# Decode attention: K of every query split by 32 dims x 4 key groups between VectorE and TensorE, V summed piece by piece

## The chip, the cores and the metric

The kernel runs on one core of a Trainium2 chip. The metric is the device time of one execution in microseconds (us), the median over several runs. The engines named below are TensorE (PE in the profile, PEld for its weight loads), VectorE (DVE), ScalarE (ACT), GpSimd (POOL) and SyncE (SP), whose queue issues all the large loads.

## The reference

One decode step for B = 2 sequences: layer norm, attention of one new token with 16 heads of 256 dims over a cache of 8192 keys, an output projection, and a bilinear feed-forward block. All is float32. The part that matters here:

```python
q = (layernorm(x) @ wq).reshape(B, 1, 16, 256).transpose(0, 2, 1, 3)
scores = jnp.einsum("bhqd,bhkd->bhqk", q, k_cache) * (256 ** -0.5)
p = softmax(scores, axis=-1)
o = jnp.einsum("bhqk,bhkd->bhqd", p, v_cache)
h = x + o.transpose(0, 2, 1, 3).reshape(B, 1, 4096) @ wo
h2 = h + ((layernorm(h) @ w_gate) * (layernorm(h) @ w_up)) @ w_down
```

k_cache and v_cache have the shape (2, 16, 8192, 256), so each of the 32 pairs of head and sequence (a "query", numbered i = 0 to 31 in the order of the loop) has 8 MB of K and 8 MB of V, and each of them is used for one vector only.

## The kernel before, in words

The host lays K, V and the weights out so that each load is one DMA of whole rows. For each query the program loads K into a tile of 128 partitions x 16384 values (64 KB a partition, line 98) and V into one of the same size (line 103). K has one buffer (`kbuf`, line 87), V has two (`vbuf`, line 88); the three fill most of the core's memory. Both loads are issued from SP's queue in the order K, V, K, V; a K load waits there until the readers of the K before it are done, and the V load behind it waits with it. The program order is as written (line 94), and each engine takes its own instructions in that order.

**V and the scores' layout.** The 8192 keys are cut into 4 groups of 2048 (`GK`), and the 256 dims into 8 pieces of 32 (`NO`, `R`). The scores of a query stand in PSUM as `s`, 128 x 2048: partition 32 g + r holds the scores of key group g, alike for all 32 values of r. There is one buffer of `s`. V's tile holds on partition 32 g + r, for each piece o, dim 32 o + r of the keys of group g, so that V times the probabilities `p` and a sum along the row gives the output, up to a sum over the four groups.

**K.** K's lower 128 dims lie one to a partition, with all 8192 keys in the row. TensorE multiplies them by the query as 32 equal columns, for each key group into its own 32 partitions of `s` (lines 266 to 272). For the upper 128 dims there are two ways. Where `by_vector(i)` holds (i a multiple of 3, and the last three; 13 of 32), they lie as V does, four pieces of 32 dims x 4 key groups; VectorE multiplies the first by the query's values (a scalar for each partition, from `qd`, line 256) and adds the other three to it with multiply-adds (line 261), the last in two halves, and TensorE then adds the 32 partitions of each group with a matmul by a block matrix of ones (line 275). The other 19 queries have the upper dims laid out as the lower and do them on TensorE, with c = 1 in line 267.

**The row of one query.** After the scores VectorE takes the maximum over `s` (line 322), ScalarE the exponential into `p` with its sum (line 324), and VectorE multiplies V by p and sums. Of three queries in turn, two do it with one multiply over all of V and one reduction (lines 346 and 347), the third with eight multiply-adds that sum as they go (line 350); `WIDE` says which, and from query 28 on all are of the second kind. ScalarE writes the query's columns for TensorE once a head (line 245).

**Around it.** Before the loop the first layer norm and the query projection run on wq, which is loaded ahead of the first K. In query 29, and again in query 31, `weights` (line 280) makes the factors that join the four groups' softmax sums, between the maximum and V. After the last V, the output projection and the feed-forward block run on weights that are loaded into the buffers of K and V as these come free (lines 359 and 366).

## Time and profile before

| | |
|---|---|
| median of 3 runs | 1303.92 us (1303.78 to 1304.15) |
| span of the profiled execution | 1302.1 us, from its first to its last instruction |
| what lies around the span, against the median | 1.8 us |
| mean granted TensorE clock | 0.647 of full speed |
| read from memory | 561.19 MB, 431 GB/s over the span |

The profiled execution has no time of its own beside the span; the 1.8 us are the difference between the median of the runs and that span. How to read the rows that the prediction shows: a group of the page gives line, engine, operation, what it writes and reads, the count, then busy time and mean duration in ns, then how long the engine stood idle just before and what ended that. A row of the timeline gives start, busy time, engine, line, operation and in brackets the idle time before it with its releaser; consecutive instructions of one kind are one row, and its time is then the sum. A row of the chain gives start, duration and the work. PEld rows are the weight loads, one ahead of each matmul, so that the distance from one to the next shows TensorE's pace. A float32 matmul shows as two instructions.

### The profile page before, as it was taken

Reading aid. Unit: us, or ns where it says so; the run is one execution under the profiler, and the core shown is the slowest. Engines: PE = TensorE matmul, PEld = TensorE weight load, DVE = VectorE, ACT = ScalarE, POOL = GpSimd, SP = SyncE. Lnnn points to the kernel's source line nnn. Section 1 sums busy time; section 2 is a strip of 40 time slices with the busy share of each in tenths; the row PEclk is TensorE's granted clock in tenths of the full one; section 3 lists DMA queues with packets and bytes.
Section 4 is the critical chain, followed back from the end, with each engine's and each line's share of the span. In section 5 each row is a group of like instructions: output and inputs, shape, how many; then the busy total and the mean of one; then the engine's idle time right before and its main releaser. Section 6 shows DMA issues by size and latency. Waiting matters only on the chain.

```text
span 1302.1 us, 5034 instructions
## 1 busy us (share of the span) xinstructions
PE 340.6 (26%) x2114; PEld 103.4 (8%) x2114; DVE 1075.6 (83%) x381; ACT 80.4 (6%) x111; POOL 2.2 (0%) x15
## 2 busy tenths in 40 slices
PE   2422112232202223211322311322311232221247
PEld 0100000000000000000000000000000000000013
DVE  0499879969987998899799879979987996987773
ACT  1100000000000000000000000000000000000000
POOL 0000000000000000000000000000000000000000
PEclk9866566666556666556666556666656666656668
DMA  9999999999999999999999999999999999999998
GB/s 419 419 449 421 447 423 445 425 443 427 439 429 441 425 441 427 437 428 437 433 435 433 434 435 435 435 433 437 431 439 431 437 429 435 433 433 433 433 425 358
DMA packets 11401, 561.50 MB, mean 431 GB/s; under 512 B 1266, under 2 KB 1652, under 8 KB 2292
## 3 DMA queue, kind: packets, MB, share of 16 engines
q1 hardware_dynamic: 11380, 561.20, 99.6%
q8 instruction: 16, 0.26, 0.1%
q14 instruction: 5, 0.04, 0.0%
HBM read 561.19 MB, written 0.00 MB: 431 GB/s over the span
## 4 chain that ended last, share of the span: by engine, by line
DMA 73%; PE 17%; DVE 10%; issue 1%; SPq 0%; DVEq 0%; ACT 0%; ACTq 0%
DMA k<-in_kc_dram 67%; PE s L269 13%; DVE k L261 6%; DMA v<-in_vc_dram 4%; PE s L275 3%; DVE v L350 3%; DMA wd_t<-in_wd_dram 2%; DVE k L256 1%; PE acc_ps L462 0%; SPq L366 0%; SPq L107 0%; PE u_ps L462 0%; SPq L98 0%; DVEq L256 0%; ACT tail L184 0%
## 5 line engine op out<-in xcount | busy, mean ns | idle before, releaser
L269 PE MATMUL s<-k,q 128*32 128x512 f32 x1632 | 248.3, 773 | 892.5 <-DMA k<-in_kc_dram 892.5
L346 DVE TENSOR_TENSOR v<-v,p 128x16384 f32<-128x16384 f32 x19 | 327.3, 17226 | 81.2 <-DMA v<-in_vc_dram 61.2
L347 DVE TENSOR_REDUCE oacc<-v 128x8 f32<-128x16384 f32 x19 | 327.2, 17220 | 0.7
L350 DVE SCALAR_TENSOR_TENSOR v<-v,p 128x2048 f32<-128x2048 f32 x104 | 231.1, 2288 | 31.8 <-ACT p L324 21.9
L269 PEld LDWEIGHTS s<-k,q 128*32 128x32 f32 x1632 | 66.7, 138 | 1070.9 <-issue 1069.2
L324 ACT ACTIVATE p<-s,nm 128x2048 f32<-128x2048 f32 x32 | 63.0, 1967 | 1131.7 <-DVE nm L322 1131.7
L322 DVE TENSOR_REDUCE nm<-s 128x1 f32<-128x2048 f32 x32 | 73.1, 2285 | 33.8 <-PE s L275 33.8
L261 DVE SCALAR_TENSOR_TENSOR k<-k,qd 128x2048 f32<-128x2048 f32 (+1 forms) x52 | 93.4, 1817 | 1.4
L275 PE MATMUL s<-k,block 128*128 128x512 f32 x104 | 48.1, 605 | 18.1 <-DVE k L261 18.1
L256 DVE TENSOR_SCALAR k<-k,qd 128x2048 f32<-128x2048 f32 x13 | 16.7, 1286 | 29.2 <-DMA k<-in_kc_dram 27.0
L275 PEld LDWEIGHTS s<-k,block 128*128 128x128 f32 x104 | 18.7, 189 | 49.0 <-DVE k L261 33.5
L138 DVE TENSOR_REDUCE sum_h_x<-xT 128x2 f32<-128x6 f32 x1 | 0.2, 159 | 20.6 <-ACT xT L165 20.6
L395 PE MATMUL acc_ps<-wo_t,oT 128*2 128x448 f32 x64 | 8.8, 646 | 11.4 <-DMA wo_t<-in_wo_dram 11.2
L201 PE MATMUL q_ps<-wq_t,xr 128*32 128x512 f32 x64 | 9.6, 753 | 1.4 <-ACT xr L184 1.1
L350 DVE DVE_READ_ACCUMULATOR v<-v,p 128x1 f32 x104 | 8.6, 83 | 0.0
L201 PE MATMUL ff_ps<-gu_t,xr 128*32 128x512 f32 (+1 forms) x32 | 6.4, 913 | 0.6 <-ACT xr L184 0.6
L324 ACT ACTIVATION_READ_ACCUMULATOR p<-s,nm 128x1 f32 x32 | 6.2, 193 | 0.0
L148 PE MATMUL total_x<-sum_h_x,ones 128*128 128x2 f32 x2 | 0.6, 348 | 21.1 <-DVE sum_h_x L141 21.1
L442 DVE TENSOR_SCALAR ve<-var_h 128x1 f32<-128x1 f32 x1 | 0.2, 158 | 6.4 <-PE var_h L440 6.4
L476 DVE COPY tail<-acc_ps 2x112 f32<-2x112 f32 x1 | 0.3, 261 | 5.5 <-PE acc_ps L462 5.5
L245 ACT ACTIVATE q<-qT 128x128 f32<-128x128 f32 x16 | 4.8, 298 | 0.0
L201 PE MATMUL u_ps<-gu_t,xr 128*32 128x512 f32 (+1 forms) x32 | 3.6, 544 | 0.0
(103 smaller groups left out, 66.0 us busy)
## 6 DMA issues: line engine op xcount, KB each, us to landing
wq_t<-in_wq_dram SPq DMA_DIRECT2D x1, 7172.0 KB, 19.6
wo_t<-in_wo_dram SPq DMA_DIRECT2D x1, 3584.0 KB, 16.5
wo_t<-in_wo_dram SPq DMA_DIRECT2D x1, 2688.0 KB, 22.5
gu_t<-in_B_w_gate_dram SPq DMA_DIRECT2D x1, 1792.0 KB, 28.0
gu_t<-in_B_w_up_dram SPq DMA_DIRECT2D x1, 1792.0 KB, 34.5
gu_t<-in_B_w_gate_dram SPq DMA_DIRECT2D x1, 1344.0 KB, 30.7
wd_t<-in_wd_dram SPq DMA_DIRECT2D x1, 1120.0 KB, 16.8
wo_t<-in_wo_dram SPq DMA_DIRECT2D x1, 896.0 KB, 24.2
```

The costliest lines, as they stand in the source:

```text
L201: nc.tensor.matmul(ps[32 * g : 32 * g + 32, : wide[g]], xs.rearrange("p b r -> p (b r)"), w[:, at : at + wide[g]], start=(c == 0), stop=(c ...
L245: nc.scalar.activation(q.rearrange("p c b r -> p (c b) r"), qT.rearrange("p k g j c b -> p (k g j) (c b)")[:, h, :, None] .to_broadcast([P ...
L256: nc.vector.tensor_scalar(upper[:, 0], upper[:, 0], qd[:, 0, i : i + 1], None, op0=ALU.mult)
L261: nc.vector.scalar_tensor_tensor(upper[:, 0, at], upper[:, o, at], qd[:, o, i : i + 1], upper[:, 0, at], op0=ALU.mult, op1=ALU.add,)
L269: nc.tensor.matmul(s[g * R : (g + 1) * R, at], q[:, c, i % B, :], kt[:, c, g, at], start=(c == 0), stop=(c == 1), skip_group_check=True,)
L275: nc.tensor.matmul(s[:, at], block, upper[:, 0, at], start=False, stop=True, skip_group_check=True,)
L322: nc.vector.tensor_reduce(nm[:, i : i + 1], s, axis=AX.X, op=ALU.max, negate=True)
L324: nc.scalar.activation(p, s, AF.Exp, bias=nm[:, i : i + 1], scale=1.0, accum_out=ls[:, i : i + 1])
L346: nc.vector.tensor_mul(v, v, p[:, None, :].to_broadcast([P, n, GK]))
L347: nc.vector.tensor_reduce(oacc[:, i, :n], v, axis=AX.X, op=ALU.add)
L350: nc.vector.scalar_tensor_tensor(v, v, 1.0, p, op0=ALU.mult, op1=ALU.mult, accum_out=oacc[:, i, o : o + 1])
L395: nc.tensor.matmul(acc_ps[32 * j : 32 * j + B, :], oT[:, h, c, :], wo_t[:, k * D : (k + 1) * D], start=(h < 2 and j > 0), stop=(h >= H - 2 ...
```

## The change

All of K now lies as V does: eight pieces of 32 dims x 4 key groups, for every query. Of the eight, the first `direct(i)` go to TensorE: two for most queries, one where i % 3 is 2 (queries 2, 5, ... 29). VectorE multiplies piece number `direct(i)` by the query's values and adds the remaining five or six to it, the last in two halves. TensorE multiplies its own pieces by a 128 x 128 matrix that holds the query's values in the blocks (`stationary`, built by ScalarE from `block`, one for each piece, ahead of each query), and closes with the matmul by ones on VectorE's sum. V is always done with eight multiply-adds, and `WIDE` is gone. `qd` now holds all eight pieces of each query, with eight small matmuls ahead of it instead of four. The sizes of the loads and their order are as before.

```diff
-WIDE = (8, 8, 0)
-def by_vector(i):
-    return i % 3 == 0 or i >= NQ - 3
+DIRECT = 2
+def direct(i):
+    return DIRECT - 1 if i % 3 == 2 else DIRECT
...
-        t = kbuf.tile([P, 2, G, GK], F32, tag="k", align_bytes=512, name=f"k_{h}_{b}")
+        t = kbuf.tile([P, NO, GK], F32, tag="k", align_bytes=512, name=f"k_{h}_{b}")
...
+    for c in range(2):
+        for o in range(G):
+            nc.tensor.matmul(
+                qd_ps[:, c * G + o, :].rearrange("p (n b) -> p n b", b=B),
...
+    def stationary(i):
+        t = work.tile([P, DIRECT, P], F32, tag="q", name=f"q_{i}")
+        for o in range(direct(i)):
+            nc.scalar.activation(t[:, o], block, AF.Copy, scale=qd[:, o, i : i + 1])
+        return t
...
     def scores(s, q, i, kt):
+        n = direct(i)
+        total = kt[:, n]
+        nc.vector.tensor_scalar(total, total, qd[:, n, i : i + 1], None, op0=ALU.mult)
+        half = GK // 2
+        steps = [(o, slice(GK)) for o in range(n + 1, NO - 1)]
+        for o, at in (*steps, (NO - 1, slice(half)), (NO - 1, slice(half, GK))):
+            nc.vector.scalar_tensor_tensor(
+                total[:, at], kt[:, o, at], qd[:, o, i : i + 1], total[:, at],
+                op0=ALU.mult, op1=ALU.add,
+            )
         tiles = [slice(j * MM, (j + 1) * MM) for j in range(GK // MM)]
+        for o in range(n):
             for at in tiles:
                 nc.tensor.matmul(
+                    s[:, at], q[:, o], kt[:, o, at], start=(o == 0), stop=False,
                     skip_group_check=True,
                 )
+        for at in tiles:
+            nc.tensor.matmul(
+                s[:, at], block, total[:, at], start=False, stop=True,
+                skip_group_check=True,
+            )
...
-        if b == B - 1 and h + 1 < H:
-            q_now = queries(h + 1)
+        if i + 1 < NQ:
+            q_now = stationary(i + 1)
...
-        n = WIDE[i % 3] if i < EARLY - B else 0
-        if n:
-            v = vt[:, :n, :]
-            nc.vector.tensor_mul(v, v, p[:, None, :].to_broadcast([P, n, GK]))
-            nc.vector.tensor_reduce(oacc[:, i, :n], v, axis=AX.X, op=ALU.add)
-        for o in range(n, NO):
+        for o in range(NO):
```

The host's layout of K follows, and the host sets a smaller scratch area for DMAs issued by GpSimd, of which the kernel has none.

VectorE's instructions, first before the change: queries 1, 2 and 3, from the maximum of query 1. In the names, the first number of a K or V tile is the sequence and the last is a running number of the program.

```order
L322 TENSOR_REDUCE nm<-s_229 128x1
L346 TENSOR_TENSOR v_1_227<-v_1_227,p_263 128x16384
L347 TENSOR_REDUCE oacc<-v_1_227 128x8
L322 TENSOR_REDUCE nm<-s_273 128x1
L350 SCALAR_TENSOR_TENSOR v_0_271,oacc<-v_0_271,p_307 128x2048 x8
L256 TENSOR_SCALAR k_1_317<-k_1_317,qd 128x2048
L261 SCALAR_TENSOR_TENSOR k_1_317<-k_1_317,qd 128x2048 x2
L261 SCALAR_TENSOR_TENSOR k_1_317<-k_1_317,qd 128x1024 x2
L322 TENSOR_REDUCE nm<-s_321 128x1
L346 TENSOR_TENSOR v_1_319<-v_1_319,p_348 128x16384
```

The same engine after the change: queries 1 and 2.

```order
L253 TENSOR_SCALAR k_1_233<-k_1_233,qd 128x2048
L257 SCALAR_TENSOR_TENSOR k_1_233<-k_1_233,qd 128x2048 x4
L257 SCALAR_TENSOR_TENSOR k_1_233<-k_1_233,qd 128x1024 x2
L316 TENSOR_REDUCE nm<-s_237 128x1
L339 SCALAR_TENSOR_TENSOR v_1_235,oacc<-v_1_235,p_258 128x2048 x8
L253 TENSOR_SCALAR k_0_270<-k_0_270,qd 128x2048
L257 SCALAR_TENSOR_TENSOR k_0_270<-k_0_270,qd 128x2048 x5
L257 SCALAR_TENSOR_TENSOR k_0_270<-k_0_270,qd 128x1024 x2
L316 TENSOR_REDUCE nm<-s_274 128x1
L339 SCALAR_TENSOR_TENSOR v_0_272,oacc<-v_0_272,p_292 128x2048 x8
```

Every query now has the same row on VectorE: K, the maximum, V, with four full steps in K or five.

TensorE's instructions, first before the change: queries 2 (all on TensorE) and 3 (upper half from VectorE), with what each waits for.

```order
L269 MATMUL s_273<-k_0_269,q_265 32x512 [waits DMAHW5_49,PE_49,Activation_49]
L269 MATMUL s_273<-k_0_269,q_265 32x512 x31
L269 MATMUL s_321<-k_1_317,q_265 32x512 [waits DMAHW7_49,Activation_49]
L269 MATMUL s_321<-k_1_317,q_265 32x512 x15
L275 MATMUL s_321<-k_1_317,block 128x512 [waits DVE_49]
L275 MATMUL s_321<-k_1_317,block 128x512
L275 MATMUL s_321<-k_1_317,block 128x512 [waits DVE_49]
L275 MATMUL s_321<-k_1_317,block 128x512
```

The same engine after the change: query 2, with one piece of its own, and query 3, with two.

```order
L264 MATMUL s_274<-k_0_270,q_260 128x512 [waits DMAHW5_49,PE_49,Activation_49]
L264 MATMUL s_274<-k_0_270,q_260 128x512 x3
L269 MATMUL s_274<-k_0_270,block 128x512 [waits DVE_49]
L269 MATMUL s_274<-k_0_270,block 128x512
L269 MATMUL s_274<-k_0_270,block 128x512 [waits DVE_49]
L269 MATMUL s_274<-k_0_270,block 128x512
L264 MATMUL s_309<-k_1_305,q_294 128x512 [waits DMAHW7_49,PE_49,Activation_49]
L264 MATMUL s_309<-k_1_305,q_294 128x512 x3
L264 MATMUL s_309<-k_1_305,q_294 128x512 [waits Activation_49]
L264 MATMUL s_309<-k_1_305,q_294 128x512 x3
L269 MATMUL s_309<-k_1_305,block 128x512 [waits DVE_49]
L269 MATMUL s_309<-k_1_305,block 128x512
```

Each query on TensorE is now four or eight matmuls that need only the load and ScalarE's matrix, and four that wait for VectorE's two halves.

## The prediction

> **What bounds the kernel now.** I read the page first: the share of the DMA queue, the chain that ended last, and the groups.

> ```profile
> PE 340.6 (26%) x2114; PEld 103.4 (8%) x2114; DVE 1075.6 (83%) x381; ACT 80.4 (6%) x111; POOL 2.2 (0%) x15
> ...
> q1 hardware_dynamic: 11380, 561.20, 99.6%
> ...
> DMA 73%; PE 17%; DVE 10%; issue 1%; SPq 0%; DVEq 0%; ACT 0%; ACTq 0%
> ...
> L346 DVE TENSOR_TENSOR v<-v,p 128x16384 f32<-128x16384 f32 x19 | 327.3, 17226 | 81.2 <-DMA v<-in_vc_dram 61.2
> ```

> The one queue of big loads is occupied for 99.6% of the span, so the loads set the pace. VectorE is next at 83%, and it still has waits (81.2 us before the wide multiplies, most for V). Next I took the stretch from the first query's K to the last one's, and a query inside it, as windows (span, busy time of PE, PEld, DVE, ACT, POOL, clock, DMA share, GB/s).

> ```profile
> 39.75:1240.37 1200.62, 289.17 (x1703) 83.53 (x1703) 1040.63 (x328) 68.89 (x83) 0.00 (x0) 0.63 1.00 434
> 504.79:543.45 38.66, 9.91 (x40) 2.99 (x40) 30.00 (x8) 2.06 (x2) 0.00 (x0) 0.63 1.00 434
> ```

> The ends of the long row are the first multiply of K for queries 0 and 31, so 31 queries take 1200.62 us, 38.73 each, and DMA never rests. One query's K and V are two loads of 19.37.

> Then the timeline of query 12, whose K has VectorE's help, and of query 14, whose V is summed piece by piece as all will be.

> ```profile
> 504.79 1.29 DVE L256 TENSOR_SCALAR k<-k,qd 128x2048 f32<-128x2048 f32 x1 [0.91 <-DMA k<-in_kc_dram]
> ...
> 506.11 7.25 DVE L261 SCALAR_TENSOR_TENSOR k<-k,qd 128x2048 f32<-128x2048 f32 x4
> ...
> 512.22 3.70 PE L275 MATMUL s<-k,block 128*128 128x512 f32 x8 [1.11 <-DVE k L261]
> ...
> 515.95 0.33 SPq L98 DMA_DIRECT2D k<-in_kc_dram  x1
> 515.96 2.29 DVE L322 TENSOR_REDUCE nm<-s 128x1 f32<-128x2048 f32 x1 [2.60 <-PE s L275]
> ...
> 597.74 2.28 DVE L322 TENSOR_REDUCE nm<-s 128x1 f32<-128x2048 f32 x1
> ...
> 602.21 2.29 DVE L350 SCALAR_TENSOR_TENSOR v<-v,p 128x2048 f32<-128x2048 f32 x1 [2.19 <-ACT p L324]
> ...
> 619.91 0.08 DVE L350 DVE_READ_ACCUMULATOR v<-v,p 128x1 f32 x1
> ```

> K has one buffer: the next K load is issued at 515.95, when TensorE has read the last of this K, 11.16 us after this K was touched. V's load has 19.37 us to run from there on, so the reload is some 8 us early and the DMA queue stays full. That margin, not VectorE's share, is what I watch. On VectorE a query is a strict row: K, a wait for TensorE (2.60), the maximum, a wait for the exponential (2.19), V.

> **The change part by part.** V: 19 queries lose a multiply of 17.23 us and a reduction over as many elements, and get eight multiply-adds. From 602.21 to 619.91 + 0.08 that is 17.78; with 0.05 to the next instruction, 17.83.

> K: every query now gets VectorE's sum. The steps' pace is in the chain of query 12:

> ```profile
> 506.11 2.36 DVE k L261
> 508.49 2.36 DVE k L261
> 510.88 1.30 DVE k L261
> ...
> 512.22 3.71 PE s L275 x8
> ```

> A full step starts 2.385 after the one before. Today one multiply, two full steps and two halves put the maximum 515.96 - 504.79 = 11.17 after K's start. With two pieces left to TensorE there are four full steps: 11.17 + 2 x 2.385 = 15.94. With one piece (every third query, ten in all) there are five: 18.33. Both carry over the 2.60 wait. The queries that had all of K on TensorE lose that burst and its early release; nothing waited for it, as the queue was full. In SP's queue V's load stands right behind K's and goes when K's goes: the buffer that it needs, of V two queries back, is free by then.

> So VectorE's row for one query, K's start to next K's start, is 15.94 + 4.47 (597.74 to 602.21) + 17.83 = 38.24 us with two pieces, and 18.33 + 4.47 + 17.83 = 40.63 with one. This is the whole argument: each step of that row needs the one before it, VectorE has them in this order for every query, and it now stands beside 38.73 of the loads. The two-piece query just fits under the loads, so I price it at 38.73; the one-piece query does not, and cannot be caught up, since its neighbours have only 0.49 to give and any lateness of K's release goes into the reload.

> Is the reload itself a new wait? The cost of restarting a drained queue is seen once, at the start:

> ```profile
> 0.75 0.40 SPq L107 DMA_DIRECT2D wq_t<-in_wq_dram  x1
> ...
> 20.37 0.21 ACT L165 ACTIVATE xT<-wq_t 128x8 f32<-128x8 f32 x1 [17.78 <-DMA wq_t<-in_wq_dram]
> ...
> 38.27 0.28 ACT L241 ACTIVATE qd<-qd_ps 128x128 f32<-128x128 f32 x1 [1.23 <-PE qd_ps L235]
> ...
> wq_t<-in_wq_dram SPq DMA_DIRECT2D x1, 7172.0 KB, 19.6
> ```

> 7172 KB at K's pace (8192 KB in 39.75 - 20.37 = 19.38) are 16.97 us, so bytes moved from 3.4, 2.65 after the issue. With two pieces the release at 15.94 plus 2.65 is 18.6, still before V's end at 19.37: no gap. With one piece, 18.33 + 2.65 + 19.37 = 40.35, just under VectorE's 40.63. So the restart costs nothing beside VectorE, by 0.3 us only.

> TensorE's clock: the direct products are 16 instructions (two pieces; a matmul shows as two) or 8 (one piece), as K lands, and the closing eight come when VectorE's first half is done: at 512.22 - 504.79 + 4.77 = 12.2 and 14.6 us. The pace of weight loads shows the clock:

> ```profile
> 39.75 0.23 PEld L269 LDWEIGHTS s<-k,q 128*32 128x32 f32 x8 [1.63 <-ACT q L245]
> 40.61 0.22 PEld L269 LDWEIGHTS s<-k,q 128*32 128x32 f32 x4 [0.62 <-issue]
> ...
> 42.84 0.14 PEld L269 LDWEIGHTS s<-k,q 128*32 128x32 f32 x4 [0.30 <-issue]
> 43.27 0.13 PEld L269 LDWEIGHTS s<-k,q 128*32 128x32 f32 x4 [0.29 <-issue]
> ...
> 736.68 0.23 PEld L269 LDWEIGHTS s<-k,q 128*32 128x32 f32 x8 [30.88 <-issue]
> ...
> 741.80 0.22 PEld L269 LDWEIGHTS s<-k,q 128*32 128x32 f32 x4 [0.63 <-issue]
> ...
> 47.19 3.70 PE L275 MATMUL s<-k,block 128*128 128x512 f32 x8 [2.44 <-DVE k L261]
> ...
> 1268.12 0.11 PEld L395 LDWEIGHTS acc_ps<-wo_t,oT 128*2 128x2 f32 x8 [9.82 <-DMA wo_t<-in_wo_dram]
> 1268.83 0.15 PEld L395 LDWEIGHTS acc_ps<-wo_t,oT 128*2 128x2 f32 x4 [0.60 <-issue]
> ...
> 1271.56 0.10 PEld L395 LDWEIGHTS acc_ps<-wo_t,oT 128*2 128x2 f32 x4 [0.35 <-issue]
> 1271.94 0.10 PEld L395 LDWEIGHTS acc_ps<-wo_t,oT 128*2 128x2 f32 x4 [0.28 <-issue]
> ```

> After a long rest TensorE takes 0.855 a step, and 0.43 once the clock has come up, 3.1 us later at the earliest (42.84); the row at 741.80 is still slow, in a burst that began at 736.68, so 6 us happen too. A gap of 2.44 us left the clock up (eight instructions in 3.70 at 47.19); a gap of 9.5 to 9.8 lost it (1268.12 to 1271.56 at 0.74, then 0.38). With one piece the 8 instructions take 5.0 to 6.84 and the gap is 7.7 to 9.6: nearest to the 9.5 row, so the closing eight start slow. Slow for 3.1 us costs 1.55; all eight slow cost 8 x 0.427 = 3.4; I take the middle, 2.5. With two pieces the direct part lasts 6.84 plus 1.55 to 3.2, the gap is 2.2 to 3.8, and I take the 2.44 row: no cost.

> [...]

> So a one-piece query costs 40.63 + 2.5 = 43.1, and its reload moves with it.

> Small terms. Query 0 has a table load of 1.28 before its exponential (38.24 + 1.28 = 39.5, 0.8 over the loads). Four more small matmuls for qd (today ready at 38.27 + 0.28) eat the 1.2 us before K lands at 39.75: 0.1. The copies that build TensorE's weights (0.3 each on ScalarE) lie beside V's 17.8: nothing; without that cover, 0.6 a query. Query 29 runs the softmax factors between maximum and V:

> ```profile
> 1174.36 2.29 DVE L322 TENSOR_REDUCE nm<-s 128x1 f32<-128x2048 f32 x1 [2.60 <-PE s L275]
> ...
> 1180.44 0.19 DVE L302 TENSOR_TENSOR w<-w,rl 128x30 f32<-128x30 f32 x1
> ...
> 1200.23 0.41 DVE L306 TENSOR_TENSOR oacc<-oacc,w 128x240 f32<-128x240 f32 x1
> ```

> 6.27 instead of 4.47, and 0.5 for line 306: 2.3, hidden by V's load today. At the end, query 31 has such factors too: its V starts 15.94 + 6.27 = 22.2 after its K at most, instead of 1259.63 - 1240.37 = 19.26, so the last layers start 2.9 later against their weights; of that, waits for weights take up 1.7:

> ```profile
> 1259.63 2.29 DVE L350 SCALAR_TENSOR_TENSOR v<-v,p 128x2048 f32<-128x2048 f32 x1 [2.30 <-DMA v<-in_vc_dram]
> ...
> 1291.61 0.16 PEld L201 LDWEIGHTS u_ps<-gu_t,xr 128*32 128x32 f32 x6 [0.40 <-DMA gu_t<-in_B_w_up_dram]
> ...
> 1296.44 0.09 PEld L462 LDWEIGHTS acc_ps<-wd_t,hmT 128*2 128x2 f32 x4 [0.37 <-DMA wd_t<-in_wd_dram]
> ...
> 1298.06 0.09 PEld L462 LDWEIGHTS acc_ps<-wd_t,hmT 128*2 128x2 f32 x4 [0.93 <-DMA wd_t<-in_wd_dram]
> ```

> 1.2 remain.

> The sum for queries 0 to 30: 21 x 38.73 + 10 x 43.1 + 0.8 + 2.3 = 1247.4 against 1200.6, so 46.8 more. After each one-piece query the next K lies ready the 0.3 us that its reload has in hand, so ten two-piece queries need about 0.25 less than 38.73: 2.5 off. With 0.1 at the start and 1.2 at the end, 45.6. The profiled span is 1302.1, and the median 1303.9 lies 1.8 above it, which I carry over: 1303.9 + 45.6 = 1349.5 us.

> **The rivals.** About 0.2%, 2.6 us, is what a measurement of this kernel can tell from no change.

> The clock stays up everywhere: one-piece queries at 40.63, 25 us less, 1324.5. For it: no gap between 2.5 and 9.5 us is on record. Against: 7.7 is nearer to the long one. 0.12.

> The clock is lost with two pieces too: 38.24 + 2.5 = 40.74, that is 2.0 over the loads in 21 queries, 42 more: 1391.5. For it: the upper end of the gap, 3.8, is past the 2.44 row. Against: it needs the gap's long end each time. 0.12. [...]

> The restart of the queue is dearer than 2.65 seen at the cold start: at 4 us a one-piece query takes 18.33 + 2.5 + 4 + 19.37 = 44.2 (1.1 more) and a two-piece one 39.3 (0.6 more): 11 + 13 = 24, so 1373.5. 0.08.

> Not slower: VectorE's busy time goes by busy share. Its work per query is 1.29 + 4 or 5 x 2.35 + 2.56 + 2.29 + 17.8, or 33.3 and 35.7, under the loads' 38.7; if the two waits in its row (2.60 and 2.19) found other work or shrank, the loads would go on setting the pace, and the time would be 1303.9, or a little less with fewer waits for V. It decides where the one-piece row falls below 38.73, 1.9 us less than the rows say, with the clock kept. Against: the order after the change puts the maximum right behind K and V right behind the maximum, and both waits stand in rows of today. 0.06, of which 0.02 faster and 0.04 the same.

> **How the numbers follow.** The forecast has 0.62, its own range 1340 to 1359 by the clock's ends (10 x 0.95 each way). Reaching from the first rival to the dear restart, with two us on either side, 1322 to 1376, holds 0.62 + 0.12 + 0.08 = 0.82. Faster 0.02, same 0.04, slower 0.94.

> **What would show it.** Right: the queue's share near 96% (99.6% x 1302 / 1348), K's first multiply waiting for VectorE's own V rather than for the load in many queries, 31 queries in about 1245 us, the wait before the maximum near 2.6 with two pieces and near 5 with one, the closing eight at 0.855. Wrong: K's first multiply still waiting for its load in every query with the queue full (the loads still bind), two-piece closings at 0.855, or steps of K or V at another pace than 2.385 and 2.21.

## The result and the profile after

The median after is 1371.16 us (1369.16 to 1373.18, four runs) against 1303.95 (1303.78 to 1304.15) before: a ratio of 1.0516, 95% interval 1.0501 to 1.0531. So it is slower, by 67.2 us where 45.6 were forecast. The profiled execution is the quickest of the four, with a span of 1367.3.

The page of the kernel after: busy time by engine, the queue of the large loads, the shares of the chain that ended last, and the groups that answer to those shown of before.

```profile
PE 464.3 (34%) x1074; PEld 186.2 (14%) x1074; DVE 1094.1 (80%) x816; ACT 93.1 (7%) x149; POOL 2.2 (0%) x15
...
q1 hardware_dynamic: 11380, 561.20, 96.0%
...
DVE 56%; DMA 26%; PE 13%; ACT 3%; issue 1%; SPq 0%; DVEq 0%; ACTq 0%
...
L339 DVE SCALAR_TENSOR_TENSOR v<-v,p 128x2048 f32<-128x2048 f32 x256 | 568.9, 2285 | 66.8 <-ACT p L318 66.8
...
L269 PE MATMUL s<-k,block 128*128 128x512 f32 x256 | 164.9, 805 | 165.1 <-DVE k L257 165.1
L316 DVE TENSOR_REDUCE nm<-s 128x1 f32<-128x2048 f32 x32 | 73.3, 2290 | 129.6 <-PE s L269 129.6
...
L253 DVE TENSOR_SCALAR k<-k,qd 128x2048 f32<-128x2048 f32 x32 | 41.0, 1283 | 23.9 <-DMA k<-in_kc_dram 23.9
```

Two of these groups as they were before, the maximum and K's first multiply:

```profile
L322 DVE TENSOR_REDUCE nm<-s 128x1 f32<-128x2048 f32 x32 | 73.1, 2285 | 33.8 <-PE s L275 33.8
...
L256 DVE TENSOR_SCALAR k<-k,qd 128x2048 f32<-128x2048 f32 x13 | 16.7, 1286 | 29.2 <-DMA k<-in_kc_dram 27.0
```

VectorE's busy time is almost what it was (1075.6 us before) and its share fell from 83% to 80%, yet it took the chain over from DMA: what binds is not how busy it is, but that K, maximum and V of every query now stand one behind the other, with waits in between. Those waits are in the third column: 129.6 us for the scores before the maximum (33.8 before), 66.8 for the exponential before V. For K's load VectorE waits 23.9 us, 15.7 of them in query 0; before it was 27.0 in only 13 queries, and V's load cost waits as well, which it no longer does. The queue is occupied for 96.0% instead of 99.6%.

The windows row of the kernel after, from the first multiply of K of query 0 to that of query 31 (columns as in the prediction):

```profile
39.73:1305.13 1265.40, 409.64 (x671) 162.87 (x671) 1054.57 (x761) 81.65 (x122) 0.00 (x0) 0.66 0.96 411
```

31 queries take 1265.40 us instead of 1200.62, at 411 GB/s instead of 434; the forecast was 1244.9. The timeline of the kernel after, from K's release in query 11 (one piece on TensorE) over queries 12 and 13 (two) into query 14 (one):

```profile
510.89 0.33 SPq L98 DMA_DIRECT2D k<-in_kc_dram  x1
...
533.49 1.28 DVE L253 TENSOR_SCALAR k<-k,qd 128x2048 f32<-128x2048 f32 x1 [0.33 <-DMA k<-in_kc_dram]
...
533.52 9.02 PE L264 MATMUL s<-k,q 128*128 128x512 f32 x16 [22.66 <-DMA k<-in_kc_dram]
...
545.70 3.70 PE L269 MATMUL s<-k,block 128*128 128x512 f32 x8 [3.15 <-DVE k L257]
...
549.43 0.33 SPq L98 DMA_DIRECT2D k<-in_kc_dram  x1
549.43 2.29 DVE L316 TENSOR_REDUCE nm<-s 128x1 f32<-128x2048 f32 x1 [2.60 <-PE s L269]
...
572.48 1.29 DVE L253 TENSOR_SCALAR k<-k,qd 128x2048 f32<-128x2048 f32 x1 [0.79 <-DMA k<-in_kc_dram]
...
572.52 9.99 PE L264 MATMUL s<-k,q 128*128 128x512 f32 x16 [23.12 <-DMA k<-in_kc_dram]
...
584.69 5.40 PE L269 MATMUL s<-k,block 128*128 128x512 f32 x8 [2.18 <-DVE k L257]
...
590.12 0.33 SPq L98 DMA_DIRECT2D k<-in_kc_dram  x1
590.13 2.29 DVE L316 TENSOR_REDUCE nm<-s 128x1 f32<-128x2048 f32 x1 [4.29 <-PE s L269]
...
612.79 1.28 DVE L253 TENSOR_SCALAR k<-k,qd 128x2048 f32<-128x2048 f32 x1 [0.40 <-DMA k<-in_kc_dram]
...
627.38 6.45 PE L269 MATMUL s<-k,block 128*128 128x512 f32 x8 [9.37 <-DVE k L257]
...
633.87 2.29 DVE L316 TENSOR_REDUCE nm<-s 128x1 f32<-128x2048 f32 x1 [5.35 <-PE s L269]
```

Query 12 releases K at 549.43, 15.94 us after its start, as forecast; but the next K is there only 23.05 us after that issue, and VectorE waits 0.79 for it. Query 13 closes K, that is, does the eight closing matmul instructions, in 5.40 instead of 3.70 (the granted clock was 0.50 from 585.17 to 588.58), so its wait before the maximum is 4.29 instead of 2.60. Query 14, with one piece, has TensorE idle for 9.37 us, closes in 6.45 and waits 5.35. All three effects lie within a microsecond or two of each other; the experiments had to tell how much each is worth.

Over the whole row, the ten one-piece queries of 0 to 30 take 43.06 on average. The 21 two-piece queries take 39.75, and in 13 of them the wait before the maximum is 4.17 to 5.37 instead of 2.60. That is where the miss is: (39.75 - 38.73) x 21 = 21.4, and 2.5 that the forecast took off for K lying ready. Split by their closing, the 8 that kept the clock (closing in 3.70) take 38.71 on average, as forecast, and the 13 that lost it (5.28 to 6.47) 40.40. So in this execution the whole excess lies in the queries that lost the clock; whether a kept clock would have saved all of it is another question, and the experiments answer it: about a third.

### The profile page after: what moved, and what is told of

Read it like the earlier page. It is cut to its first block, busy times and chain, and to the rows that moved or that the text cites. A ratio compares the mean times of both kernels' runs of the same rounds, so it can differ in the third digit from the quotient of the medians.

```text
span 1367.3 us, 3428 instructions
## 1 busy us (share of the span) xinstructions
PE 464.3 (34%) x1074; PEld 186.2 (14%) x1074; DVE 1094.1 (80%) x816; ACT 93.1 (7%) x149; POOL 2.2 (0%) x15
## 3 DMA queue, kind: packets, MB, share of 16 engines
q1 hardware_dynamic: 11380, 561.20, 96.0%
## 4 chain that ended last, share of the span: by engine, by line
DVE 56%; DMA 26%; PE 13%; ACT 3%; issue 1%; SPq 0%; DVEq 0%; ACTq 0%
DVE k L257 27%; DMA k<-in_kc_dram 26%; DVE v L339 23%; PE s L269 12%; DVE nm L316 3%; DVE k L253 3%; ACT p L318 3%; PE ff_ps L201 0%; PE u_ps L201 0%; PE hT_ps L407 0%; PE ff_ps L451 0%; ACT L318 0%; PE l_ps L293 0%; PE acc_ps L451 0%; PE acc_ps L384 0%
## 5 line engine op out<-in xcount | busy, mean ns | idle before, releaser
L339 DVE SCALAR_TENSOR_TENSOR v<-v,p 128x2048 f32<-128x2048 f32 x256 | 568.9, 2285 | 66.8 <-ACT p L318 66.8
L264 PE MATMUL s<-k,q 128*128 128x512 f32 x432 | 255.5, 755 | 689.8 <-DMA k<-in_kc_dram 688.9
L257 DVE SCALAR_TENSOR_TENSOR k<-k,qd 128x2048 f32<-128x2048 f32 (+1 forms) x202 | 403.9, 2013 | 6.0
L269 PE MATMUL s<-k,block 128*128 128x512 f32 x256 | 164.9, 805 | 165.1 <-DVE k L257 165.1
L264 PEld LDWEIGHTS s<-k,q 128*128 128x128 f32 x432 | 103.6, 249 | 840.7 <-issue 839.6
L316 DVE TENSOR_REDUCE nm<-s 128x1 f32<-128x2048 f32 x32 | 73.3, 2290 | 129.6 <-PE s L269 129.6
L269 PEld LDWEIGHTS s<-k,block 128*128 128x128 f32 x256 | 63.3, 259 | 266.0 <-DVE k L257 194.3
L253 DVE TENSOR_SCALAR k<-k,qd 128x2048 f32<-128x2048 f32 x32 | 41.0, 1283 | 23.9 <-DMA k<-in_kc_dram 23.9
L339 DVE DVE_READ_ACCUMULATOR v<-v,p 128x1 f32 x256 | 20.6, 80 | 0.0
L247 ACT ACTIVATE q<-block,qd 128x128 f32<-128x128 f32 x54 | 18.9, 389 | 0.1
L201 PE MATMUL q_ps<-wq_t,xr 128*32 128x512 f32 x64 | 9.6, 752 | 1.4 <-ACT xr L184 1.1
L201 PE MATMUL ff_ps<-gu_t,xr 128*32 128x512 f32 (+1 forms) x32 | 4.9, 720 | 0.6 <-ACT xr L184 0.6
L201 PE MATMUL u_ps<-gu_t,xr 128*32 128x512 f32 (+1 forms) x32 | 3.6, 542 | 0.0
## 6 DMA issues: line engine op xcount, KB each, us to landing
wq_t<-in_wq_dram SPq DMA_DIRECT2D x1, 7172.0 KB, 19.6
wo_t<-in_wo_dram SPq DMA_DIRECT2D x1, 896.0 KB, 19.4
```

The lines of the kernel that those rows point to most:

```text
L201: nc.tensor.matmul(ps[32 * g : 32 * g + 32, : wide[g]], xs.rearrange("p b r -> p (b r)"), w[:, at : at + wide[g]], start=(c == 0), stop=(c ...
L247: nc.scalar.activation(t[:, o], block, AF.Copy, scale=qd[:, o, i : i + 1])
L253: nc.vector.tensor_scalar(total, total, qd[:, n, i : i + 1], None, op0=ALU.mult)
L257: nc.vector.scalar_tensor_tensor(total[:, at], kt[:, o, at], qd[:, o, i : i + 1], total[:, at], op0=ALU.mult, op1=ALU.add,)
L264: nc.tensor.matmul(s[:, at], q[:, o], kt[:, o, at], start=(o == 0), stop=False, skip_group_check=True,)
L269: nc.tensor.matmul(s[:, at], block, total[:, at], start=False, stop=True, skip_group_check=True,)
```

## The experiments

Two theories stood at the start. **A**: VectorE's row binds, and the difference is the clock lost in two-piece queries. **B**: the clock loss costs little there, because K's reload, behind a queue that has run dry, is late too. Times are medians, ratios against the kernel before with their 95% interval.

**V's part alone (v_pieces).** The kernel before with all of V summed piece by piece:

```diff
-WIDE = (8, 8, 0)
+WIDE = (0, 0, 0)
```

> The kernel before with V always by eight multiply-adds, K as it was: the V part of the change alone. Both theories: the loads still set the pace, since VectorE's row is then at most 11.2 + 4.5 + 17.8 = 33.5 us a query and K's release does not move; 1304 us, the same as before within 2. If VectorE's V work counted by itself, 19 queries x 16.6 us of VectorE time less would show as something faster.

1304.95 us, ratio 1.0008 (0.9999 to 1.0017): not told from no change, so the whole loss comes with K. VectorE's busy time fell to 760.9 us in this kernel, without any gain, as the loads bind.

**The clock held up (keep_both, keep_one, keep_two).** Products into a spare PSUM tile, which nobody reads before the last layers, stand between TensorE's own pieces and the closing matmuls, nine in one-piece queries and two in two-piece ones:

```diff
+SPARE = {1: 9, 2: 2}   # keep_one: {1: 9, 2: 0}; keep_two: {1: 0, 2: 2}
...
+        for m in range(SPARE[n]):
+            nc.tensor.matmul(
+                spare, q[:, 0], kt[:, 0, tiles[m % 4]], start=True, stop=True,
+                skip_group_check=True,
+            )
         for at in tiles:
             nc.tensor.matmul(
                 s[:, at], block, total[:, at], start=False, stop=True,
```

> TensorE gets idle products between its own pieces of K and the closing ones: 9 matmuls with one piece, 2 with two, into a PSUM tile that nothing reads then. They fill its gap to under 2 us. Theory A (the clock, lost in the gap, makes the closing matmuls slow in both kinds of query): the eight closing instructions take 3.70 us everywhere, the wait before the maximum is 2.60 everywhere, a one-piece query costs about 40.6 and a two-piece one 38.7, and the time falls from 1371 to about 1328 us. Theory B (the 22 us above the forecast come from restarting the drained queue, and the clock matters only with one piece): about 1349. If the clock has nothing to do with the gap: 1371.

> The idle products in the ten one-piece queries alone. Theory A: their wait before the maximum falls from 4.0 to 5.5 to 2.60, 2.2 us each, the two-piece ones stay as they are, about 1348 us (22 less than 1371). Theory B gives the same here; the run is there to price one kind against the other.

> The idle products in the 22 two-piece queries alone. Theory A: no two-piece closing is slow any more, which frees 24 us of waits, of which the loads (38.7 a query) take some back: about 1351 us. Theory B: the two-piece closings cost nothing, 1371 as before.

keep_both 1342.79 (1.0297, 1.0268 to 1.0327), keep_one 1347.9 (1.0354, 1.0317 to 1.0391), keep_two 1364.08 (1.0464, 1.0443 to 1.0484). In the groups of keep_both, VectorE's waits and the closing matmuls:

```profile
L323 DVE TENSOR_REDUCE nm<-s 128x1 f32<-128x2048 f32 x32 | 73.3, 2292 | 92.5 <-PE s L276 92.5
L276 PE MATMUL s<-k,block 128*128 128x512 f32 x256 | 127.8, 645 | 39.6 <-DVE k L259 39.4
...
L255 DVE TENSOR_SCALAR k<-k,qd 128x2048 f32<-128x2048 f32 x32 | 41.1, 1285 | 31.4 <-DMA k<-in_kc_dram 31.1
```

The wait before the maximum falls by 37.1 us, from 129.6 to 92.5 (2.9 a query, near the 2.60 of a kept clock), and the wait for K's load grows by 7.2. The one-piece part is what the forecast made of it: keep_one takes 23.3 off the median, where slow closings were priced at 25. The two-piece part is the surprise: clock lost in 13 of 21 queries, yet keep_two takes off only 7.1, and in keep_both two-piece queries still take 39.38 (39.08 in the 16 that close fast; 5 are still slow). keep_both comes out between theory A's 1328 and theory B's 1349, and keep_two between 1351 and 1371: neither theory holds alone. What a kept clock leaves over was looked for in the reload.

**Two pieces for every query (two_pieces, two_keep).** No query has the sixth step on VectorE; two_keep adds the two spare products.

```diff
 def direct(i):
-    return DIRECT - 1 if i % 3 == 2 else DIRECT
+    return DIRECT
```

> Two pieces of K on TensorE in every query, none with one. VectorE's row is then 38.24 us with the clock up, under the loads' 38.73. Theory A: some 13 of 21 in ten of the closings still start or turn slow (1.7 us), so about 1336 us. Theory B (queue restart, clock harmless with two pieces): about 1308, since with the release at 15.94 the queue never drains.

> Two pieces in every query and two idle matmuls in TensorE's gap. Theory A: no closing is slow, VectorE's row 38.24 lies under the loads' 38.73, and the loads bind again: about 1307 us, 3 over the kernel before, for the softmax factors and the table load that have no cover. Theory B: the same as with two pieces and no idle products.

two_pieces 1344.44 (1.0316, 1.0258 to 1.0374), two_keep 1339.15 (1.0275, 1.0256 to 1.0293). two_pieces lies nearer to theory A's 1336 than to B's 1308, while two_keep is not told from two_pieces (the intervals overlap), against A's 1307: each theory is right for one half. The forecast for the row alone was missed: with 29 of 31 closings fast, a query of two_keep takes 39.79 although VectorE's row is 38.24. Its queue and groups, a query on its timeline, and its windows:

```profile
q1 hardware_dynamic: 11380, 561.20, 98.5%
...
L323 DVE TENSOR_REDUCE nm<-s 128x1 f32<-128x2048 f32 x32 | 73.3, 2291 | 86.5 <-PE s L276 86.5
...
L255 DVE TENSOR_SCALAR k<-k,qd 128x2048 f32<-128x2048 f32 x32 | 41.1, 1286 | 55.8 <-DMA k<-in_kc_dram 39.7 <-ACT qd L244 16.0
```

```profile
596.52 1.29 DVE L255 TENSOR_SCALAR k<-k,qd 128x2048 f32<-128x2048 f32 x1 [1.78 <-DMA k<-in_kc_dram]
...
612.47 2.29 DVE L323 TENSOR_REDUCE nm<-s 128x1 f32<-128x2048 f32 x1 [2.60 <-PE s L276]
...
637.27 1.29 DVE L255 TENSOR_SCALAR k<-k,qd 128x2048 f32<-128x2048 f32 x1 [2.54 <-DMA k<-in_kc_dram]
```

```profile
609.00:614.00 5.00, 3.43 (x8) 1.16 (x7) 2.40 (x2) 0.00 (x0) 0.00 (x0) 1.00 1.03 406
614.00:619.00 5.00, 0.00 (x0) 0.00 (x0) 2.81 (x2) 2.64 (x4) 0.00 (x0) 0.76 0.68 275
```

VectorE is done early and waits 2.54 us for K; the query takes 40.75. K's reload went out at 612.46, 15.94 us after this K's start, when V's load still had about 3.4 of its 19.37 us to run, to 615.9 or so. Yet the bandwidth around that moment is 275 GB/s instead of 434: this reload, though it was in the queue before the load ahead of it ended, did not keep DMA full. At 434, the bytes missing in these 5 us take (1 - 275/434) x 5 = 1.8 us, and the query is 2.0 over the loads' 38.73.

**A shorter row, and an earlier reload (v_seven, k_halves, v_seven_k_halves).** v_seven leaves out V's last piece (its sums are set to zero), which makes VectorE's row 2.2 us shorter. k_halves loads K into two tiles, and VectorE and TensorE use the tiles so that the first comes free early and its reload starts long before V's load ends; TensorE's own pieces are then the last of K's.

```diff
-        for o in range(NO):
+        for o in range(NO - 1):
```

```diff
-        t = kbuf.tile([P, NO, GK], F32, tag="k", align_bytes=512, name=f"k_{h}_{b}")
-        nc.sync.dma_start(t.rearrange("p o k -> p (o k)"), kc[b, h])
+        for n in range(2):
+            t = kbuf.tile([P, G, GK], F32, tag=f"k{n}", align_bytes=512, name=f"k{n}_{h}_{b}")
+            nc.sync.dma_start(
+                t.rearrange("p o k -> p (o k)"), kc[b, h][:, n * G * GK : (n + 1) * G * GK]
+            )
...
```

> The changed kernel with seven of V's eight pieces summed; the last piece of the output is left out. VectorE's row is 2.2 us shorter in every query, K's release and its reload are where they were. If VectorE's row alone binds: 2.2 less in some 31 queries down to the loads' pace, about 1322 us. If K's late release and the restart of the queue bind just as much (release + 2.9 + 19.4 us): only 3 to 6 us less, about 1367.

> The changed kernel with K loaded as two tiles of four pieces, the first released after VectorE's first five steps; nothing else. If VectorE's row, slow closings in it, and the restart of the queue both bind at about the same length (as the run with seven pieces of V says), taking the restart away alone gives only the waits for K that the changed kernel shows, 8 us: about 1364. If the restart were the larger of the two: well below 1350.

> As the run with seven pieces of V, and K loaded as two tiles of four pieces, so that the first half is released after VectorE's first five steps (10.9 us) and its reload keeps the queue full while the second half is still read. If the restart of the queue is what binds beside VectorE's row: about 1322 us, some 45 less than with seven pieces and one tile. If it is not: the same as that run.

v_seven alone 1367.75 (1.0493, 1.0471 to 1.0514), k_halves alone 1380.37 (1.0586, 1.057 to 1.0602), both together 1311.84 (1.0067, 1.005 to 1.0083). VectorE's first multiply of K in v_seven, and in k_halves with the closing matmuls and the maximum:

```profile
L254 DVE TENSOR_SCALAR k<-k,qd 128x2048 f32<-128x2048 f32 x32 | 41.2, 1286 | 89.5 <-DMA k<-in_kc_dram 89.5
```

```profile
L277 PE MATMUL s<-k,block 128*128 128x512 f32 x256 | 185.8, 892 | 381.8 <-DVE k L265 381.8
...
L324 DVE TENSOR_REDUCE nm<-s 128x1 f32<-128x2048 f32 x32 | 73.3, 2292 | 150.5 <-PE s L277 150.5
...
L261 DVE TENSOR_SCALAR k<-k,qd 128x2048 f32<-128x2048 f32 x32 | 41.0, 1282 | 15.7 <-DMA k<-in_kc_dram 15.7
```

In v_seven, nearly all the time taken out of V (31 x 2.2 = 68 us) comes back as wait for K's load: 89.5 us instead of 23.9. The reload is thus a bound of its own, hardly shorter than the row. k_halves was a miss: expected at 1364, and slower than the change itself. Its reload is indeed early (VectorE waits for K only in query 0), but TensorE then does its own pieces at K's landing, while VectorE is still at V, and stands idle for 381.8 us in all before the closings; every closing is slow (892 ns an instruction instead of 805), and the wait before the maximum rises to 150.5. So k_halves does not show the reload's price by itself: it takes one delay away and adds another. With the two edits together 59.3 us come off, and 31 queries take 1206.3 us, near the loads' 1200.6, although the closing is slow in 20 of the 21 two-piece queries: with seven pieces of V and the early reload, slow closings cost hardly anything in this run.

**Both remedies on the change (keep_both_k_halves, two_keep_k_halves).** The spare products and the two tiles for K, in the change and with two pieces for all.

> K in two tiles and the idle products in both kinds of query: neither the clock nor the restart is left, only VectorE's row of 38.24 and 40.63. Those average 39.0 against the loads' 38.73: about 1320 us (1328 if a one-piece query's excess cannot be caught up by its neighbours). The run with the idle products alone, 1343, is then short of this by the restart.

> Two pieces everywhere, idle products and K in two tiles. If the clock, the one-piece row and the restart are all that the change costs, VectorE's row of 38.24 lies under the loads and they bind again: about 1307 us, against 1339 with K in one tile. If another cost is left in the changed K or V: above 1315.

keep_both_k_halves 1375.28 (1.0546, 1.0529 to 1.0564), a miss by some 50 us; two_keep_k_halves 1314.22 (1.0081, 1.0061 to 1.01), 7 over its 1307. A one-piece query of the former on its timeline, and the queue and the groups of the latter:

```profile
598.95 6.14 PE L274 MATMUL s<-k,q 128*128 128x512 f32 x8 [14.37 <-DMA k<-in_kc_dram]
...
604.92 7.89 PE L279 MATMUL u_ps<-k,q 128*128 128x512 f32 x18
...
606.80 1.28 DVE L263 TENSOR_SCALAR k<-k,qd 128x2048 f32<-128x2048 f32 x1
...
621.40 5.17 PE L284 MATMUL s<-k,block 128*128 128x512 f32 x8 [8.59 <-DVE k L267]
...
626.61 2.29 DVE L331 TENSOR_REDUCE nm<-s 128x1 f32<-128x2048 f32 x1 [4.07 <-PE s L284]
```

```profile
q1 hardware_dynamic: 15988, 561.20, 99.2%
...
L331 DVE TENSOR_REDUCE nm<-s 128x1 f32<-128x2048 f32 x32 | 73.3, 2291 | 89.6 <-PE s L284 89.6
```

The spare products ran at K's landing too (from 604.92, before VectorE's first multiply at 606.80) and left a gap of 8.59 us, after which the closing took 5.17 instead of 3.70. With two pieces everywhere the row is under the loads, so K does not come ahead of VectorE, the products fall where they should, and the queue is full again (99.2%). Its profiled span is 8.5 us longer than before: 31 queries take 1206.6 us instead of 1200.6 (most of it in query 0, with its table load of 1.28, query 29, with the softmax factors, and six queries at 39.5 to 39.8), and the rest after K of query 31 takes 64.4 instead of 61.7; why those six are longer was not followed up. The change itself, with its one-piece queries, was not measured with both remedies at work.

**The release alone (late_release).** In v_pieces, where VectorE is busy for 58% and the loads bind, spare products that read K after the closing matmuls hold K's release back to about 16 us after its start:

```diff
+        sizes = [MM] * 5 + [MM // 2] if by_vector(i) else [MM] * 8
+        for size in sizes:
+            nc.tensor.matmul(
+                spare[:, :size], block, kt[:, 1, 0, :size], start=True, stop=True,
+                skip_group_check=True,
+            )
```

> The kernel before, with V by multiply-adds, and idle products that read K after the closing ones, so that K is released some 15.9 us after its start in every query instead of 9 to 11; VectorE has nothing more to do than before and its row (33.5 us) has 5 us to spare. By the prediction's margin (V's load ends 19.37 after K's, restart 2.65) nothing drains: 1305. If the queue in fact drains some 16 us after K lands, as the run with two pieces and idle products shows in one place, each query loses about 1 us: 1335 to 1340.

1334.64 (1.0228, 1.0209 to 1.0247): 29.7 us more than v_pieces, 0.96 for each of 31 queries. By the prediction's margin it should have cost nothing. A query on its timeline, and a longer stretch as windows, of v_pieces and of late_release:

```profile
513.72 1.28 DVE L257 TENSOR_SCALAR k<-k,qd 128x2048 f32<-128x2048 f32 x1 [1.61 <-issue]
...
529.61 0.33 SPq L98 DMA_DIRECT2D k<-in_kc_dram  x1
...
533.40 2.29 DVE L357 SCALAR_TENSOR_TENSOR v<-v,p 128x2048 f32<-128x2048 f32 x1 [6.22 <-DMA v<-in_vc_dram]
```

```profile
513.72:1220.00 706.28, 170.80 (x996) 49.46 (x995) 424.84 (x349) 41.71 (x52) 0.00 (x0) 0.63 1.00 434
```

```profile
513.72:1220.00 706.28, 280.18 (x1249) 97.29 (x1249) 413.21 (x338) 39.06 (x46) 0.00 (x0) 0.70 0.99 422
```

K's reload is issued at 529.61, V's load ends at 533.40, 3.79 us later: more than the 2.65 of the prediction. VectorE stands waiting for V meanwhile, so its row plays no part. Still the bandwidth is 422 instead of 434 GB/s. This is the missing term by itself. Over the 16 queries whose landings are all in the trace, the issue comes 2.4 to 4.9 us ahead of the end of V's load, 3.4 on average.

## Why the prediction was right and where it failed

The direction and the mechanism held. The row of K, maximum and V is strict; where the clock was kept, the release comes 15.94 us after K's start; the steps keep their pace (2.39 us from one to the next in K, 2.21 in V), the share of the queue is the 96% that was named, in 17 of 31 queries K's first multiply does not wait for its load, and V's multiply-adds cost nothing by themselves (v_pieces, 1304.95).

The one-piece queries: 43.1 forecast, 43.06 measured (42.87 without query 29, which has the softmax factors). Their wait before the maximum is 4.85 on average, 2.25 over the 2.60 of a kept clock, where 2.5 was taken. With the factors of query 29 the forecast for the ten was 433.3, and they took 430.6.

The two-piece queries are where the prediction failed, in two steps. The first: "With two pieces the release at 15.94 plus 2.65 is 18.6, still before V's end at 19.37: no gap." The end of V's load was taken as one moment up to which DMA is full. late_release shows that a release at this point costs 0.96 a query with VectorE's work unchanged, and two_keep less two_keep_k_halves gives 24.9 us, 0.80 a query, from the other side. The second: "I take the 2.44 row: no cost." The clock was lost in 13 of 21 two-piece queries, as the second rival feared; slow closings there had been named as a sign of being wrong. The row that stood for a long gap was misread as well: at the 9.53 us gap of the kernel before, the profile has the granted clock at half from 1254.23 on, before the gap began at 1258.59, so that gap did not lose it. The gaps of about 9 us in the kernel after all led to slow closings (gaps of 8.91 to 9.65 in the ten one-piece queries, closings of 5.11 to 6.57), so the one-piece sum came out right all the same.

The two steps hide each other. A late closing delays the row and K's release alike, so either step would account for much of the miss without the other; for the slow closings alone this is argued, as no run has them without the reload's loss. In the execution that was profiled the 13 queries that lost the clock hold all of the excess (13 x 1.67 = 21.7). Yet with the clock held in 16 of the 21 keep_two takes off only 7, because the reload then binds: two-piece queries that close fast take 39.17 in keep_two and 39.76 in two_keep, not 38.73. The 8 fast ones of the kernel after reach 38.71, and 7 of them found their K ready, after a query that was late. Hence the pattern of the runs: against the change, keep_two takes off 7, v_seven 3 (not told from nothing, as the intervals overlap), k_halves, which also makes every closing slow, adds 9, and v_seven with k_halves takes off 59. The runs split the miss between the two steps no further than that.

In sums: forecast for the 21 (with query 0's 0.8) 811.6, taken 834.8. That is 23.2 more; less 2.7 from the one-piece queries, it is the 20.5 by which the 31 queries missed. The tail came out at 62.2 after 61.7, 0.7 less than forecast, and the median lies 3.9 above the profiled span instead of 1.8, as that execution was the quickest of a wider spread: 20.5 - 0.7 + 2.1, with 0.1 less at the start, gives the 21.7 to within rounding.

The rival of a dearer restart, given 0.08, came nearest in time (1373.5), but that is luck: its price did not come true. In the kernel after, six K loads whose landing is recorded were issued when V's load had already landed. Five of them landed 21.64 to 21.77 us after their issue and one 22.50 (query 12), against 19.37 in a full queue: 2.3 to 3.1 for a restart, about the 2.65 that was taken, and not 4. The two-piece loss begins before the queue is dry at all. The forecast's own 1340 to 1359 was missed by 12 us. That 1371.2 still lies inside the wide range is partly luck too, since the range reached that far only for this rival. The second rival had its mechanism right in 13 of 21 queries, but not its 42 us, as it left the reload out.

No version here beats the kernel before. Its loads already fill the queue for 99.6% of the span, so no relief of VectorE or TensorE could show.

Where the bandwidth goes can be counted in the packet records of late_release, from K's issue of query 1 to that of query 31 (1192.5 us; 1162.9 in v_pieces). The 16 DMA engines stand without a packet for 12.3 us on average (0.9 in v_pieces): some have moved their part of V's load before it has landed, with the reload already issued. The packet records of the kernel after show it for the reload issued at 302.91, 2.84 us before V's load landed: 0.75 us after the issue 3 packets were under way, where a full queue has 16, and 14 at 1.5 us. And 423 of 7695 packets of 64 KB take more than 2.6 us, up to 4.3, where 2.42 is the median in the kernels before and after; half of those start within 1.8 us behind a reload's issue, and they add 16.4 us an engine (0.6). Together that is 27.2 of the 29.6 us more. Why these packets take longer stays open.

## What to carry to other kernels

Where one buffer is reloaded behind another load, don't count its margin up to the end of that load as a whole: measure it by delaying the release alone, with work that only reads the buffer. When two bounds stand side by side within a few per cent, taking away either one tells almost nothing; take away both before judging a theory. And an earlier load is not only a gain: it moves whatever starts at its landing, here TensorE's products, away from the work that closes them.

## What the runs showed of the hardware

```profile
537.38:540.79 3.41, 3.41 (x9) 1.00 0.78 332
540.79:544.21 3.42, 1.75 (x5) 1.00 1.11 479
544.21:547.62 3.41, 1.93 (x5) 1.00 0.98 423
547.62:551.03 3.41, 1.77 (x5) 1.00 0.76 327
```

```profile
578.34:581.75 3.41, 3.41 (x9) 1.00 0.84 365
581.75:585.17 3.42, 1.24 (x3) 1.00 0.84 364
585.17:588.58 3.41, 3.41 (x5) 0.50 1.24 538
588.58:591.99 3.41, 1.51 (x4) 1.00 0.89 308
```

Query 12's gap is split over two steps that are each busy for 0.51 to 0.57, and the clock stays; query 13's lies in one step, busy for 0.36, and the next step is at half clock. Counted over the whole steps between the first multiplies of K of queries 0 and 31: before the change, the 31 steps at full clock that were followed by half clock were busy for 0.24 at most, and the 60 followed by full clock for 0.43 at least; after it, 54 for 0.45 at most and 67 for 0.42 at least. Of the steps at half clock, the 30 before and 54 after that were followed by full clock were busy for 0.81 or more, and the 228 and 193 followed by half clock for 0.78 or less. In these two executions the busy share of a step thus separates kept from lost almost without overlap, and the length of a gap does not: of the 21 two-piece queries, the eight that kept the clock had gaps of 2.96 to 3.22 us; of the thirteen that lost it, four had gaps of 1.89 to 2.52 and nine of 3.24 or more. The difference is worth 1.69 us a query (40.40 against 38.71).

What a reload costs that comes shortly before the load ahead of it ends was new as well: 0.96 us a query, with loads of 8 MB, for issues 2.4 to 4.9 us ahead (late_release). In the kernel before, K's reloads are issued 8.0 to 10.7 us before V's load lands, and a query takes the 38.73 of its two loads.
